# One step less per unit in the chunks, another list of ramp steps, GpSimd in written order from chunk 10 on, the count ahead of the last copies

## The chip, the cores and the metric

The kernel runs on one core of a Trainium2 chip. The metric is the device time of one execution in microseconds, as the median of several runs. An interval or a range of runs stands beside it where there is one.

## What is computed

Three layers follow one another. The first is a recurrence over 768 time steps for each of 4 x 8 heads with a state of 40 x 40; it is shown below with its loop. Its output, 3072 rows of 320 numbers, goes through an expert layer of three products with weights of 320 x 768, of which the largest is taken element by element, and a product back to 320. The last layer has weights of 320 x 2048 and back, with `h * tanh(softplus(h))` between.

```python
for t in range(S):                       # S = 768, heads of 40 x 40
    y[:, :, t] = np.einsum('bhd,bhde->bhe', rt, state)
    Sa = np.einsum('bhde,bhe->bhd', state, at)
    state_decay = state * wt[:, :, None, :] - np.einsum('bhd,bhe->bhde', Sa, bt)
    state = state_decay + np.einsum('bhd,bhe->bhde', vt, kt)
...
h = np.maximum(np.maximum(x @ w1, x @ w2), x @ w3)      # moe1
x = h @ w_out
...
h = x @ w_in                                            # moe2
sp = np.where(h > 20.0, h, np.log1p(np.exp(np.minimum(h, 20.0))))
out = (h * np.tanh(sp)) @ w_out
```

Weights and inputs arrive as 64-bit numbers and are converted on the chip. A value that a product multiplies is held as a high and a low part (names in h and l: bxh and bxl, hh and hl, gh and gl), so that one product of the text is three or more matmuls.

## The kernel before

**The units of work.** The recurrence runs in 48 chunks, c0 to c47. Two successive chunks make a unit, n. `Attention.pre(n)` prepares a unit in steps: each `yield` ends a step, and whoever drives the unit takes one step at a time. The steps are, in order: a scan on VectorE; logarithm and exponential on ScalarE; two steps of VectorE and two more that scale bk; two steps of matmuls (L328) into one PSUM bank of the pool ps_un; the copy ab on ScalarE (L333), which reads half of that bank; the transpose akT on VectorE (L336), which reads the other half; and four selects on GpSimd (L343), which read akT. The transposes kb on TensorE (L388) take banks of the same pool, four to a bank; ScalarE copies them out (L392).

**The solves.** Four units make a batch, and `solve(k)` inverts the triangles of batch k. From the third batch on these are 62 operations on GpSimd, in 31 pairs of a product (L371) and a subtraction (L373), after a transpose on VectorE (L364). For the first two they run on VectorE. `Attention.run` deals the pairs out to the slots that are left until the batch is due.

**The chunks and moe1.** A chunk has five slots. In each, `run` takes a step of the chunk's chain (`chain(c)`, which begins with the copy L452; its TensorE products are cgps, L416, its VectorE copies ud, L464), steps of `moe1.group`, the next unit's steps and steps of the solve. `moe1.group` belongs to four chunks: matmuls bps (L743 to L747), the maximum mx (L873, L875), its high part hh on ScalarE (L877) and its low part hl on GpSimd (L878), which waits for hh; then the output products L916, which need hl, and a copy of the result out (L905, L907). The input bxl is made on VectorE (L756) from the chain's output. L248 is a scaling of ax on GpSimd, and L281 the scan of a later unit.

**What sets the order.** Chunks c0 to c8 come from START, a list of steps that is written out by hand, one token a step: u0 is a step of unit 0, c3 one of chunk 3's chain, e1 one of the solve of batch 1, w5 one of weight tile 5's conversion, f20 a slot of moe1, k6 half of a unit's kb, and further letters are loads and clears. In this ramp all engines keep the written order. From chunk 9 on `run` writes the order; TensorE, VectorE, ScalarE and the DMA queue of SyncE keep it, and GpSimd alone is left to the scheduler:

```python
does = dict(u=unit, x=self.mult, c=chain, e=substitute, ...
...
for x in START.split():
...
                with tc.manual_schedule(engines=IN_ORDER | {mybir.EngineType.Activation}):
                    finish(chunks)
```

**moe2 and the end.** After chunk 47 the rest of moe2's weights is converted, and six groups, `group(q)`, run products (L1093 to L1095), the activation and the products back, in the scheduler's order on every engine. The last group's result leaves in four copies, two on ScalarE and two on VectorE, and two output transfers. Then `gate.count` adds up numbers that ScalarE collected on the way (one matmul, one VectorE reduction and one cast), every engine loads the result into a register (L176) and branches on it (L1363): a slow general version would run only if inputs lay out of bounds.

Of the kernel before, what the change touches and what calls it, by code (L numbers as in the profile page):

```python
# [102 lines left out]
u0 u2 u2 u0 u0 u0 u1 u1 x2 u0 u0 u1 u1 L0 u1 u1 u1 u3 x3 u3 u2 u2 u2 u2 u2 u2 u1 u1 u2 u3 u3 u3 l2 u3 u3 w3 u2
w0 u2 u3 w0 u3 w1 w4 z5 A5 e0 L1 w1 u3 z6 A6 D w2 u3 e0 e0 e0 w5 z4 e0 e0 w1 e0 e0 w3 w0 r V1 e0 z7 A7 A4 e0
w3 e0 w2 e0 e0 w0 e0 e0 w6 e0 e0 K4 K5 U w3 e0 e0 w1 e0 w4 e0 e0 e0 e0 w5 e0 e0 w6 w7 k0 w3 w5 w2 w2 k1 w5 w4
w4 w4 w6 w8 w5 e0 e0 e0 e0 e0 e0 e0 e0 Z0 c0 w7 K6 w7 w6 c0 u4 w8 u4 c0 w9 w6 w10 w8 Z1 x4 w11 w12 w9 c0 w7 u4
u4 w8 V2 c0 w11 w9 w13 u4 u5 w7 L2 w9 c1 A8 w8 w9 w10 w11 w10 k2 w14 w12 w10 u4 u5 x5 c1 w15 u5 w10 w11 u4 u4
w12 w16 c1 w13 w11 w12 w14 c1 w13 w17 w14 u4 w18 u4 w15 w13 c1 u5 w12 k3 V3 w14 u5 K7 w13 w15 w19 w14 u4 w16
u5 L3 w17 w17 u5 c2 w15 w16 w20 c2 u5 w18 c2 w15 w18 w19 u5 w17 w21 u5 c2 V4 c2 w18 k4 w17 u5 w19 w19 w20 c3
w18 w22 w23 w20 L4 w20 K8 w21 c3 w23 w19 w20 c3 w21 w23 w22 k5 w21 c3 w22 w23 w23 A9 u6 w21 V5 w16 c3 w16 L5  # L110
x6 w22 w22 c4 f20 u6 u6 c4 f21 u6 c4 u6 u6 u7 u7 c4 u7 V6 x7 f22 u6 u7 c4 K9 u7 u6 u6 u6 u6 L6 c5 f23 u7 u7 u7
f24 f25 u7 e1 c5 f26 A10 u7 e1 e1 e1 e1 e1 c5 f27 c5 V7 f28 u7 e1 e1 e1 e1 c5 f29 k6 k7 e1 c6 c6 f30 c6 e1 e1
L7 e1 e1 e1 f31 e1 e1 e1 c6 V8 e1 e1 e1 c6 k8 e1 f32 f33 e1 u8 u8 e1 L8 e1 e1 x8 c7 A11 e1 f34 u8 f35 e1 e1 u8
c7 f36 u8 u8 e1 e1 c7 u8 u8 e1 u9 x9 u8 u9 f37 u8 e1 c7 u9 f38 u8 u9 c7 f39 V9 k9 L9 u9 K10 u9 u10 u10 u9 x10
c8 f40 u10 u10 c8 f41 u9 u9 u9 c8 f42 u10 u11 x11 u9 c8 f43 K11 u10 c8 f44 u10 V10 u11 u11 L10
# [1267 lines left out]
```

## Time and profile before

| what | value |
|---|---|
| median of 3 runs | 1033.3 us (1029.38 to 1034.28) |
| the profiled execution, its own time | 1034.91 us |
| the span of its profile | 1033.2 us |
| mean granted TensorE clock | 0.967 |
| TensorE (PE) busy | 917.4 us, 89% |
| VectorE (DVE) busy | 752.2 us, 73% |
| ScalarE (ACT) busy | 735.3 us, 71% |
| GpSimd (POOL) busy | 479.4 us, 46% |

The span runs from the first to the last instruction that the profile holds; the execution's own time is 1.7 us longer. Busy time is summed over an engine's instructions. It is an average over three stages: the ramp (about 0 to 189 us), the chunks (to about 634 us) and moe2 (to the end). A granted clock of 1.0 is 2.4 GHz on TensorE and 0.5 is 1.2 GHz.

### The profile page before, as it was taken

To read this page: it belongs to the slowest core of one execution; us is meant where nothing else is said; L and a number is where in the kernel's file an instruction comes from. 1 tells how busy PE (TensorE), PEld (TensorE's weight loads), DVE (VectorE), ACT (ScalarE), POOL (GpSimd) and SP (SyncE) were. 2 spreads that over 40 slices of the span, in tenths; PEclk is the share of its full clock that TensorE was granted. 3 is DMA by queue.
4 is the path that set the end of the run, shared out by engine and by line. 5 is a ranking of instruction groups with operands and counts; after the bars stand their busy time and mean duration, and the time that the engine had idled before them with its cause. 6 is when DMAs were issued, how large, how long until landed. Compare 5 with 4: busy or idle time off the path is not lost. (4 is left out here: it accounts for less than half of the span.)

```text
span 1033.2 us, 34141 instructions
## 1 busy us (share of the span) xinstructions
PE 917.4 (89%) x14098; PEld 824.6 (80%) x14098; DVE 752.2 (73%) x1411; ACT 735.3 (71%) x1858; POOL 479.4 (46%) x715
## 2 busy tenths in 40 slices
PE   3046778899999999999999999979999999999996
PEld 3034667798888888898988988969888999889985
DVE  8976788665564656565366666698998888898875
ACT  5466635575765667576688977878787978878874
POOL 8488706479659838963953434880202010020000
PEclk9999588899999999999999999989999999999999
DMA  9565522535354454445345454420100000000000
GB/s 233 148 182 160 134 51 65 152 95 150 92 139 118 114 148 106 118 113 139 94 129 151 124 140 150 118 66 1 57 1 31 26 32 26 24 33 1 26 1 29
DMA packets 117334, 96.07 MB, mean 93 GB/s; under 512 B 73316, under 2 KB 93412, under 8 KB 117172
## 3 DMA queue, kind: packets, MB, share of 16 engines
q1 hardware_dynamic: 116432, 93.59, 33.4%
q8 instruction: 113, 1.85, 0.8%
q14 instruction: 49, 0.40, 0.1%
q10 hardware_dynamic: 740, 0.23, 0.1%
HBM read 81.20 MB, written 12.58 MB: 91 GB/s over the span
## 5 line engine op out<-in xcount | busy, mean ns | idle before, releaser
L743 PE MATMUL bps<-bxh,bw 128*128 128x256 f32 x432 | 140.6, 326 | 4.5 <-ACT mx L873 3.4
L744 PE MATMUL bps<-bxl,bw 128*128 128x256 f32 x432 | 124.9, 289 | 3.1 <-DVE bxl L756 3.1
L745 PE MATMUL bps<-bxh,bw 128*128 128x256 f32 x432 | 123.7, 286 | 0.0
L1046 POOL CAST cxh<-cxl 128x512 fp32r<-128x512 f32 x15 | 13.1, 911 | 188.2 <-DMA cxl<-x 188.2
L743 PEld LDWEIGHTS bps<-bxh,bw 128*128 128x128 f32 x432 | 83.4, 193 | 13.3 <-ACT mx L873 4.0
L744 PEld LDWEIGHTS bps<-bxl,bw 128*128 128x128 f32 x432 | 84.2, 195 | 4.9 <-DVE bxl L756 4.9
L248 POOL TENSOR_TENSOR ax<-ax,pp 40x256 f32<-40x256 f32 x96 | 69.2, 739 | 37.1 <-DVE pp L281 24.0
L745 PEld LDWEIGHTS bps<-bxh,bw 128*128 128x128 f32 x432 | 84.1, 195 | 0.0
L483 DVE TENSOR_TENSOR rs<-cgps,cst 64x256 f32<-64x256 f32 x96 | 40.6, 423 | 58.2 <-PE cgps L416 56.1
L878 POOL TENSOR_TENSOR hl<-mx,hh 128x256 fp32r<-128x256 f32 x72 | 56.0, 779 | 52.6 <-ACT hh L877 46.4
L1089 DVE TENSOR_TENSOR gl<-e,gh 128x512 fp32r<-128x512 f32 x93 | 69.9, 752 | 14.4 <-ACT gh L1088 13.4
L500 DVE TENSOR_TENSOR sv<-ys,pp 40x320 f32<-40x320 f32 x92 | 44.9, 488 | 47.3 <-PE ys L495 45.8
L875 DVE TENSOR_TENSOR mx<-bps,mx 128x256 f32<-128x256 f32 x144 | 60.2, 418 | 24.6 <-ACT mx L873 13.7
L373 POOL TENSOR_TENSOR T<-T,tv 128x31 f32<-128x31 f32 (+15 forms) x124 | 73.7, 594 | 8.6
L916 PE MATMUL bps<-hh,bo 128*128 128x256 f32 x360 | 77.0, 296 | 0.6 <-ACT mx L873 0.6
L1077 ACT ACTIVATE e<-e 128x512 f32<-128x512 f32 x93 | 58.6, 630 | 25.4 <-DVE e L1075 25.0
L1081 DVE SCALAR_TENSOR_TENSOR e<-e,r 128x512 f32<-128x512 f32 x93 | 68.6, 737 | 8.7 <-ACT r L1079 8.6
L495 PE MATMUL ys<-rs,ls 128*40 128x72 f32 x1536 | 66.9, 247 | 8.5 <-DVE rs L483 4.2
L371 POOL TENSOR_TENSOR tv<-tr,T 128x31 f32<-128x31 f32 (+15 forms) x124 | 67.8, 547 | 11.1 <-DVE tr L364 2.6
L343 POOL TENSOR_SCALAR_AFFINE_SELECT ax<-akT 32x256 f32<-32x256 f32 x96 | 47.5, 494 | 51.5 <-DVE akT L336 47.3
L495 PEld LDWEIGHTS ys<-rs,ls 128*40 128x40 f32 x1536 | 58.0, 130 | 15.1 <-issue 4.9
L1074 ACT ACTIVATE e<-cps 128x512 f32<-128x512 f32 x93 | 54.7, 589 | 18.9 <-PE cps L747 18.8
(241 smaller groups left out, 3157.2 us busy)
## 6 DMA issues: line engine op xcount, KB each, us to landing
bk<-in_KB_dram SPq DMA_DIRECT2D x24, 448.0 KB
sv<-in_SV_dram SPq DMA_DIRECT2D x96, 80.0 KB
raw<-in_w_dram SPq DMA_DIRECT2D x18, 384.0 KB
again<-in_w_dram SPq DMA_DIRECT2D x27, 256.0 KB
w<-in_W_dram SPq DMA_DIRECT2D x21, 231.0 KB
v<-in_VT_dram SPq DMA_DIRECT2D x48, 96.0 KB
rs<-in_RT_dram SPq DMA_DIRECT2D x48, 96.0 KB
cxl<-x SPq DMA_DIRECT2D x12, 384.0 KB
```

Of the source, the lines that this page charges most:

```text
L248: self.nc.gpsimd.tensor_tensor(out=xv[:, h], in0=xv[:, h], in1=P[ro, h, 0:C], op=ALU.mult)
L371: eng.tensor_tensor(out=tv, in0=abT[:, s, s + 1:C].unsqueeze(2).to_broadcast([128, n, s + 1]), in1=T[:, s, 0:s + 1].unsqueeze(1).to_broadc ...
L373: eng.tensor_tensor(out=T[:, s + 1:C, 0:s + 1], in0=T[:, s + 1:C, 0:s + 1], in1=tv, op=ALU.subtract)
L495: nc.tensor.matmul(out=self.ys[64 * y:64 * y + 40, p, 0:72], lhsT=l[:, y, p], rhs=r_[:, :, 4 * (p % 4) + 2 * (1 - y) + p // 4], start=True ...
L743: nc.tensor.matmul(out=ps, lhsT=h[:, k], rhs=xh[:, k], start=(k == 0), stop=False)
L744: nc.tensor.matmul(out=ps, lhsT=h[:, k], rhs=xl[:, k], start=False, stop=False)
L745: nc.tensor.matmul(out=ps, lhsT=l[:, k], rhs=xh[:, k], start=False, stop=False)
L875: after(1, lambda ps=ps, mx=mx: nc.vector.tensor_tensor(out=mx, in0=ps, in1=mx, op=ALU.max))
L916: nc.tensor.matmul(out=pss[d][rows], lhsT=lhsT, rhs=rhs, start=first, stop=last)
L1077: nc.scalar.activation(out=e, in_=e, func=AF.Square, bias=1.0)
L1081: nc.vector.scalar_tensor_tensor(out=e, in0=e, scalar=1.0, in1=r, op0=ALU.add, op1=ALU.mult)
L1089: nc.vector.tensor_tensor(out=gl, in0=e, in1=gh.bitcast(F32), op=ALU.subtract)
```

## The change

It has four parts.

1. In `pre`, the step between the copy ab and the transpose akT exists only while the ramp is written out (`self.written`). After it, both stand in one step, so akT and the selects come one step earlier.
2. START is another list. It holds the same 472 steps as the one before, in another order. In chunk 9, which `run` writes, the loads of the tests are fixed in order only from there on (`free`).
3. From chunk 10 on (past HAND, 9), a chunk whose number is a multiple of 4 takes no solve steps in its first slot, and from the end of the ramp on GpSimd too keeps the written order.
4. In the last moe2 group, products 13 to 15 are issued one tile earlier; `count` runs ahead of the final copies and takes a bank of the pool psa; three of those copies go to ScalarE and one to VectorE; the second output transfer is issued on ScalarE's queue.

```diff
 START = """
-m0 m1 K0 W0 W1 A0 W2 m2 A2 A1 K1 W3 K2 m3 A3 s1 V0 K3 w0 w1 w2 l1 s0 C l0 p R1 R0 u0 u0 u1 x0 u1 x1 u0 u0 u0
+W0 m1 m2 m0 W1 A2 A0 W2 K0 W3 V0 A1 K1 s0 K2 C m3 A3 s1 K3 w0 w1 w2 l1 p u0 u1 x0 u0 R0 u0 u0 u1 u0 u0 u0 R1
...
-    def count(self):
+    def count(self, psum):
...
-        with self.tc.tile_pool(name="g_ps", bufs=1, space=PSUM) as ps:
-            p = ps.tile([1, len(runs)], F32, name="g_p")
...
+        p = psum[0:1, 0:len(runs)]
+        nc.tensor.matmul(out=p, lhsT=ones, rhs=cnt, start=True, stop=True)
...
         nc.scalar.copy(out=self.ab[:, i:i + 8], in_=psv[:, :, C:2 * C])
-        yield
+        if self.written:
+            yield
         akT = p1.tile([128, 4, 2, C], F32, name="akT")
...
                     steps = -(-left // max(1, 5 * (due - c) - slot - 2))
+                    if c > HAND and c % 4 == 0 and slot == 0:
+                        steps = 0
...
-            self.tc.keep_in_program_order(dma)
+            if self.free:
+                self.tc.keep_in_program_order(dma)
...
+        last = q == 5
...
+        made = {p for r, p in self.ps if r == q}
         for m in range(16 + 3):
-            if early <= m < 16 and (q, m) not in self.ps:
-                self.product(q, m)
+            for p in (m, m + 1)[:1 + (last and m >= 12)]:
+                if early <= p < 16 and p not in made:
+                    self.product(q, p)
+                    made.add(p)
...
+        if last:
+            self.passed = self.gate.count(self.psa.tile([128, self.N], F32, name="cps"))
...
-                if i:
+                if i and not (last and b2):
                     nc.vector.tensor_copy(out=o[:, j], in_=acc[j])
...
-            nc.sync.dma_start(out=self.out[r0:r0 + 2 * GT]...
+            (nc.scalar if last and b2 else nc.sync).dma_start(out=self.out[r0:r0 + 2 * GT]...
...
-                    if c >= HAND and (c > HAND or slot > 0) and slot in (1, 4):
+                    if c >= 9 and (c > 9 or slot > 0) and slot in (1, 4):
...
-                with tc.manual_schedule(engines=IN_ORDER | {mybir.EngineType.Activation}):
+                moe1.free = True
+                with tc.manual_schedule(engines=IN_ORDER | {mybir.EngineType.Activation, mybir.EngineType.Pool}):
...
-    n, total = gate.count()
+    n, total = moe2.passed
```

How the instructions move is shown at three places. The line numbers of the changed kernel are shifted by up to 5: its L883 is L878 of before, its L912 is L907, its L880 is L875, its L247 is L248, and its L745 to L749 are L743 to L747.

**GpSimd, the end of a moe1 group in the chunks (near 330 us).** hl are the low parts that the output products wait for; the rows on T and tv are a solve. Before:

```order
L373 TENSOR_TENSOR T_161<-T_161,tv 128x18x14
L248 TENSOR_TENSOR ax_142<-ax_142,pp_155 40x256 x4
L371 TENSOR_TENSOR tv<-tr_173,T_161 128x255
L878 TENSOR_TENSOR hl_6590<-mx,hh_6584 128x256
L373 TENSOR_TENSOR T_161<-T_161,tv 128x17x15
L371 TENSOR_TENSOR tv<-tr_173,T_161 128x256
L373 TENSOR_TENSOR T_161<-T_161,tv 128x16x16
L371 TENSOR_TENSOR tv<-tr_173,T_161 128x255
L373 TENSOR_TENSOR T_161<-T_161,tv 128x15x17
L878 TENSOR_TENSOR hl_6591<-mx,hh_6585 128x256
L371 TENSOR_TENSOR tv<-tr_173,T_161 128x252
```

With the change, the same stretch of the solve:

```order
L373 TENSOR_TENSOR T_161<-T_161,tv 128x19x13
L371 TENSOR_TENSOR tv<-tr_173,T_161 128x252
L373 TENSOR_TENSOR T_161<-T_161,tv 128x18x14
L883 TENSOR_TENSOR hl_6592<-mx,hh_6586 128x256
L371 TENSOR_TENSOR tv<-tr_173,T_161 128x255
L373 TENSOR_TENSOR T_161<-T_161,tv 128x17x15
L883 TENSOR_TENSOR hl_6593<-mx,hh_6587 128x256
L371 TENSOR_TENSOR tv<-tr_173,T_161 128x256
L373 TENSOR_TENSOR T_161<-T_161,tv 128x16x16
L371 TENSOR_TENSOR tv<-tr_173,T_161 128x255
L373 TENSOR_TENSOR T_161<-T_161,tv 128x15x17
```

The last hl of the group stood behind the pair of operations on 16 x 16 and the pair on 15 x 17. It now stands ahead of both, one pair after the hl before it. The names' numbers are counted otherwise: hl_6593 of after is hl_6591 of before.

**VectorE in the chunks, around a unit's akT (near 290 us).** L907 copies out a result of moe1, L464 is a copy of the chain. Before:

```order
L502 TENSOR_TENSOR YT<-ys,pp_158 104x8x32
L755 TENSOR_SCALAR bxh,g_t<-bxl 128x768
L756 TENSOR_TENSOR bxl<-bxl,bxh 128x768
L907 TENSOR_TENSOR mx<-bps,mx 64x256
L336 STREAM_TRANSPOSE akT<-m_3558 128x2x4x32
L464 COPY ud<-ups 128x4x40
L281 SCALAR_TENSOR_TENSOR pp_157<-w,rst 104x528
```

With the change:

```order
L502 TENSOR_TENSOR YT<-ys,pp_158 104x8x32
L757 TENSOR_SCALAR bxh,g_t<-bxl 128x768
L758 TENSOR_TENSOR bxl<-bxl,bxh 128x768
L336 STREAM_TRANSPOSE akT<-m_3558 128x2x4x32
L912 TENSOR_TENSOR mx<-bps,mx 64x256
L464 COPY ud<-ups 128x4x40
L280 SCALAR_TENSOR_TENSOR pp_157<-w,rst 104x528
```

akT stood behind L907 and now stands ahead of it; the rows above and below keep their order.

**TensorE in chunk 9, just past the ramp.** L388 are the transposes kb, L743 to L747 a group of moe1 products, L472 and L416 are of the chain. Before:

```order
L746 MATMUL bps<-bxh,bw_107 128x256
L747 MATMUL bps<-bxl,bw_107 128x256
L472 MATMUL utps<-cst,ud 128x128 x2
L743 MATMUL bps<-bxh,bw_108 128x256
L744 MATMUL bps<-bxl,bw_108 128x256
L745 MATMUL bps<-bxh,bw_108 128x256
L743 MATMUL bps<-bxh,bw_108 128x256
L744 MATMUL bps<-bxl,bw_108 128x256
L745 MATMUL bps<-bxh,bw_108 128x256
L746 MATMUL bps<-bxh,bw_108 128x256
L747 MATMUL bps<-bxl,bw_108 128x256
L388 MATMUL kb<-cst,bk_150 128x104 x8
```

With the change:

```order
L388 MATMUL kb<-cst,bk_150 128x104 x4
L472 MATMUL utps<-cst,ud 128x128 x2
L745 MATMUL bps<-bxh,bw_108 128x256
L746 MATMUL bps<-bxl,bw_108 128x256
L747 MATMUL bps<-bxh,bw_108 128x256
L745 MATMUL bps<-bxh,bw_108 128x256
L746 MATMUL bps<-bxl,bw_108 128x256
L747 MATMUL bps<-bxh,bw_108 128x256
L748 MATMUL bps<-bxh,bw_108 128x256
L749 MATMUL bps<-bxl,bw_108 128x256
L388 MATMUL kb<-cst,bk_150 128x104 x4
L416 MATMUL cgps<-rs_167,uT 32x32
```

The eight transposes stood in one row behind the products. Four of them now stand ahead of L472 and of the products, and four behind these.

## Rows read from the trace of the kernel before

**Rows 1.** The page, busy time of each engine over the span.
```profile
PE 917.4 (89%) x14098; PEld 824.6 (80%) x14098; DVE 752.2 (73%) x1411; ACT 735.3 (71%) x1858; POOL 479.4 (46%) x715
```

**Rows 2.** Busy time by stretch: us, each engine (x), PEclk, DMA share, GB/s.
```profile
123.00:158.00 35.00, 26.50 (x504) 23.76 (x504) 30.88 (x76) 13.62 (x41) 7.63 (x13) 0.80 0.26 57
...
290.00:339.00 49.00, 46.53 (x1017) 42.58 (x1018) 28.53 (x53) 31.27 (x97) 41.69 (x66) 0.93 0.45 119
...
740.00:1000.00 260.00, 260.00 (x1436) 234.09 (x1435) 226.54 (x373) 216.80 (x373) 22.19 (x18) 1.00 0.07 23
```

**Rows 3.** Waits of TensorE from 189 to 634 us: total, times, longest.
```profile
PE kb L388 <- DVE akT L336: 4.7, 6, 1.0
...
PE bps L916 <- POOL hl L878: 3.2, 3, 1.5
...
PE cgps L416 <- ACT uT L475: 2.5, 3, 1.4
```

**Rows 4.** Busy time and granted clock (PEclk) of two short stretches, as in rows 2.
```profile
197.00:203.80 6.80, 6.17 (x130) 5.46 (x132) 1.87 (x4) 3.13 (x10) 2.70 (x6) 0.50 0.32 89
...
425.70:429.10 3.40, 3.40 (x56) 3.04 (x45) 0.78 (x2) 0.00 (x0) 3.02 (x5) 0.50 0.15 46
```

**Rows 5.** Timeline near 290 us: start, length, instruction [idle before <-what ended it].
```profile
289.59 0.36 ACT L333 COPY ab<-m 128x256 f32<-128x256 f32 x1
...
291.09 0.42 DVE L907 TENSOR_TENSOR mx<-bps,mx 64x256 f32<-64x256 f32 x1 [1.13 <-ACT mx L905]
...
291.55 0.45 DVE L336 STREAM_TRANSPOSE akT<-m 128x256 f32<-128x256 f32 x1
...
292.15 0.55 PE L388 MATMUL kb<-cst,bk 104*128 104x104 f32 x4 [1.02 <-DVE akT L336]
```

**Rows 6.** Timeline near 330 us, GpSimd (POOL) and TensorE.
```profile
328.08 0.62 POOL L371 TENSOR_TENSOR tv<-tr,T 128x256 f32<-128x256 f32 x1
...
330.93 0.72 POOL L878 TENSOR_TENSOR hl<-mx,hh 128x256 fp32r<-128x256 f32 x1
...
331.70 0.38 PE L916 MATMUL bps<-hl,bo 128*128 128x256 f32 x1 [1.42 <-POOL hl L878]
```

**Rows 7.** Groups of GpSimd by line in the chunks; lengths ns min/median/max of akT, hl.
```profile
L373 POOL TENSOR_TENSOR T<-T,tv 128x31 f32<-128x31 f32 (+15 forms) x124 | 73.7, 594 | 8.6
...
L371 POOL TENSOR_TENSOR tv<-tr,T 128x31 f32<-128x31 f32 (+15 forms) x124 | 67.8, 547 | 11.1 <-DVE tr L364 2.6
...
L343 POOL TENSOR_SCALAR_AFFINE_SELECT ax<-akT 32x256 f32<-32x256 f32 x57 | 29.5, 517 | 43.6 <-DVE akT L336 41.4
...
L336 DVE STREAM_TRANSPOSE akT<-m x14: 439/441/451, 194.1 to 477.9; 128x256 f32<-128x256 f32 x14
...
L878 POOL TENSOR_TENSOR hl<-mx,hh x59: 722/734/1687, 201.6 to 631.6; 128x256 fp32r<-128x256 f32 x59
```

**Rows 8.** Timeline of chunk 9 near 197 us.
```profile
194.56 0.57 PE L388 MATMUL kb<-cst,bk 104*128 104x104 f32 x4 [0.64 <-DVE akT L336]
...
196.73 0.85 ACT L392 COPY ls<-kb 64x320 f32<-64x320 f32 x2
...
197.63 0.95 PE L388 MATMUL kb<-cst,bk 104*128 104x104 f32 x4 [2.50 <-ACT ls L392]
```

**Rows 9.** Timeline of the end.
```profile
1023.16 0.41 PE L1093 MATMUL cops<-c_cw,gh 128*128 128x320 f32 x1 [1.34 <-ACT gh L1088]
...
1024.44 0.75 PE L1095 MATMUL cops<-c_cw,gl 128*128 128x320 f32 x4
...
1026.54 0.14 DVE L175 CAST g_n<-g_s 1x1 int32<-1x1 f32 x1
```

**Rows 10.** Register load (L176) and branch (L1363) by engine: lengths ns min/median/max.
```profile
L176 PEldq TENSOR_LOAD <-g_n x1: 1033/1033/1033, 1026.7 to 1026.7; - x1
...
L1363 ACTq COMPARE_BRANCH  x1: 50/50/50, 1027.7 to 1027.7; - x1
...
L1363 PEldq COMPARE_BRANCH  x1: 4012/4012/4012, 1027.9 to 1027.9; - x1
```

More of the change, by code (lines that the diff above doesn't have):

```diff
@@ L101 @@
 START = """
-m0 m1 K0 W0 W1 A0 W2 m2 A2 A1 K1 W3 K2 m3 A3 s1 V0 K3 w0 w1 w2 l1 s0 C l0 p R1 R0 u0 u0 u1 x0 u1 x1 u0 u0 u0
[L103 to L115, printed above, removed]
+W0 m1 m2 m0 W1 A2 A0 W2 K0 W3 V0 A1 K1 s0 K2 C m3 A3 s1 K3 w0 w1 w2 l1 p u0 u1 x0 u0 R0 u0 u0 u1 u0 u0 u0 R1
@@ new lines @@
+u2 x1 u2 l0 u1 u1 u2 u0 x2 u1 u1 u0 u1 u0 u0 u1 u1 u3 x3 u3 l2 u2 u2 u2 L0 u1 u3 u1 u3 z6 u3 u3 u2 u2 u2 u3 w0
+w3 L1 u2 u2 u3 w1 w1 u3 e0 w0 w4 w5 u3 z4 u3 z5 w2 K4 e0 A5 e0 w1 e0 e0 e0 A6 z7 e0 U A4 e0 w0 w0 A7 w2 w3 e0
+e0 w6 e0 e0 e0 w1 w4 w3 w3 w5 K5 e0 e0 e0 e0 e0 e0 w3 e0 e0 e0 w7 w2 w2 w4 w4 w5 w4 w6 e0 k0 k1 e0 w6 D w8 w5
+e0 w5 r K6 w9 w10 e0 V1 e0 e0 e0 e0 e0 e0 e0 e0 c0 w7 w7 Z0 c0 u4 w8 w8 u4 c0 w9 w11 w12 x4 w7 c0 u4 u4 w9 Z1
+w8 V2 w13 w11 c0 u4 w7 w8 L2 w9 c1 A8 w6 w11 w6 u5 w10 w10 u4 k2 w12 w10 x5 w13 u5 u5 u5 w10 w12 u4 u4 w14 w11
@@ new lines @@
+w11 w13 c1 c1 w9 c1 w15 w16 w17 u4 u4 w13 w13 V3 w14 w14 w18 w12 k3 w12 u5 u5 w15 c1 L3 w17 w15 w19 w14 w16 c2
+c2 w14 u4 w15 w18 w18 u5 c2 w17 w19 u5 w15 w16 w20 w21 c2 V4 w19 w18 u5 w17 u5 w19 w20 w18 u5 w22 w17 c2 k4
+w23 w20 c3 A9 L4 c3 w20 w21 w23 w19 w21 c3 w20 w22 w23 w22 w22 w21 k5 w23 c3 V5 w21 u6 w16 w22 w16 c3 L5 w23
+K7 c4 f20 u6 u6 c4 x6 u6 c4 u6 f21 u6 u7 u7 K8 c4 u7 u7 u6 c4 L6 u6 u7 u6 u6 x7 V6 u6 c5 u7 u7 u7 f22 f23 u7
+A10 f24 f25 K9 c5 u7 u7 e1 e1 e1 e1 e1 e1 c5 c5 e1 f26 f27 e1 e1 e1 V7 f28 k6 c5 L7 e1 e1 e1 e1 c6 c6 e1 c6 e1
@@ L116 @@
+k7 c6 e1 e1 e1 f29 e1 e1 f30 e1 c6 L8 f31 f32 u8 f33 e1 e1 u8 e1 e1 c7 A11 f34 f35 e1 u8 u8 x8 V8 e1 e1 e1 u8
+u8 c7 e1 e1 f36 c7 u8 u8 u8 e1 u9 x9 u9 u8 f37 k8 e1 c7 u9 V9 f38 u8 u9 c7 K10 f39 u9 u9 u10 x10 u10 u10 u9 c8
+L9 f40 c8 u10 u9 u9 f41 u9 u10 u11 c8 f42 x11 c8 V10 f43 u10 k9 K11 c8 u9 u10 f44 u11 u11 L10
 """
@@ L168, in count @@
         nc.vector.memset(ones, 1.0)
-        with self.tc.tile_pool(name="g_ps", bufs=1, space=PSUM) as ps:
-            p = ps.tile([1, len(runs)], F32, name="g_p")
-            nc.tensor.matmul(out=p, lhsT=ones, rhs=cnt, start=True, stop=True)
-            s = pool.tile([1, 1], F32, name="g_s")
-            nc.vector.tensor_reduce(out=s, in_=p, op=ALU.add, axis=mybir.AxisListType.X)
+        p = psum[0:1, 0:len(runs)]
+        nc.tensor.matmul(out=p, lhsT=ones, rhs=cnt, start=True, stop=True)
+        s = pool.tile([1, 1], F32, name="g_s")
+        nc.vector.tensor_reduce(out=s, in_=p, op=ALU.add, axis=mybir.AxisListType.X)
         n = pool.tile([1, 1], I32, name="g_n")
@@ L802, in weights @@
             yield from64(self.nc, self.tmp, self.A["wo"][j], 1, DM, self.gate, lambda t, j=j: self.put_out(t[:, 0], j), later=True)
+    free = False
     def tests(self):
@@ L1133, in group @@
             r0 = (2 * ga + b2) * S + sb * GT
-            nc.sync.dma_start(out=self.out[r0:r0 + 2 * GT].rearrange("(i p) d -> p i d", i=2), in_=o[:, b2:4:2])
+            (nc.scalar if last and b2 else nc.sync).dma_start(out=self.out[r0:r0 + 2 * GT].rearrange("(i p) d -> p i d", i=2), in_=o[:, b2:4:2])
 def any64(nc, pool, src, n, cols, out):
```

## The prediction

> **What bounds the kernel now.** I read the page first, then busy time by stretch, then who makes TensorE wait in the chunks, then the granted clock behind those waits, and last the end of the program instruction by instruction. TensorE is busy for 89% of the span [rows 1]. By stretch it falls into three parts [rows 2]. In the ramp no engine is full for long; VectorE comes nearest, with 30.88 of 35 us from 123 to 158 us, where the second solve runs on it. In the chunks TensorE is the bound: 46.53 of 49 us from 290 to 339 us, with GpSimd second at 41.69. In the closing stage TensorE is simply full, 260.00 of 260 us. So a wait of TensorE in the chunks is worth its own length, while in the ramp only the chain through the list counts.
>
> In the chunks TensorE's waits are few and have names [rows 3]: the transposes kb (L388) wait for VectorE's akT, 4.7 us in six places; the output products L916 wait for GpSimd's hl, 3.2 us in three; cgps (L416) waits for ScalarE's uT, 2.5 us. One kb waits 2.50 us for ScalarE's copies of the kb before it [rows 8]. The reader should add what comes behind some of them: near 197, 262, 293, 334 and 426 us, each time within two and a half microseconds of such a wait, the granted clock stands at 0.50, that is 1.2 GHz, for 6.8 us the first time and 3.4 us the other four, with TensorE nearly full [rows 4], which shows the first and the last of the five. At half the rate 3.4 us do the work of 1.7, so such a stretch costs 1.7 us beside the wait, the long one 3.4.
>
> **The change, part by part.**
>
> *akT one step earlier.* akT now shares its slot with ab, the ScalarE copy that empties the same bank. Before, VectorE took L907 first; L907 waited for ScalarE until 291.09 us, akT followed at 291.55, and kb came 1.02 us late, although ab had begun at 289.59 [rows 5]. After, akT stands ahead of L907, so it need not wait for what L907 waits for. No instruction is added. L907 becomes later by akT's length, 0.45 us; behind it is an output transfer, for which TensorE does not wait. At most all six waits go, 4.7 us, and the clock stretch near 293, 1.7 us; at least nothing. I take 4.1 + 1.7 = 5.8 us, and leave out the wait of 0.64 us at 194.56 [rows 8], the one of the six in the part that the list reorders.
>
> *GpSimd in written order, and no solve steps in the first slot of every fourth chunk.* The last hl of a group stood behind four solve operations, the first of them at 328.08 us; it ran at 330.93 us and TensorE's product came 1.42 us late [rows 6]. Now it stands ahead of those four: a lead of 330.93 - 328.08 = 2.85 us against a wait of 1.42. One group later the same pattern costs the longest wait of its row, 1.5 us [rows 3]. Both waits go, 2.9 us, with their two clock stretches, 3.4 us: 6.3 us, at least nothing. The solve operations left out of that slot go to others. Counted from the order, two successive chunks held up to 26 of them on GpSimd and now hold 20 in the steady pattern; at 0.57 us each, the mean of their two lines [rows 7], the fullest pair gives up 6 x 0.57 = 3.4 us of GpSimd work. A pair lasts (477.9 - 194.1) / 13 = 21.8 us by the starts of akT [rows 7]. That is why I expect no new queue in the steady pattern. The first solve in the chunks keeps 26 operations in a pair, and there, near 259 us, an hl that holds back ScalarE now stands behind more work than before: for the uT wait I count nothing.
>
> *The list of ramp steps.* It holds the same 472 steps, so the engines do the same work. Until the first solve ends VectorE has the same seven weight conversions ahead of it, so chunk 0 starts when it did, and up to chunk 7 VectorE's work only moves from one chunk to the next. I take 0, and as bounds 8 us either way, twice the 4 us that VectorE is idle in the stretch of rows 2. One edit is plain: in chunk 9 eight kb transposes stood in a row on one bank, and the second four waited 2.50 us until ScalarE had copied the first four, which it did only at 196.73 us [rows 8]. They now stand apart, with a group of products between them. That wait and the 6.8 us at half clock would go: 2.5 + 3.4 = 5.9 us, at least nothing; I take it all.
>
> *The end.* TensorE waited 1.34 us for the last gh [rows 9]. In the last group, products 13 to 15 are now issued one tile early, so ScalarE and VectorE get their inputs earlier while TensorE's own work stays: I take 1.2 us, bounds 0 and 1.34. After that, TensorE's last products ended at 1024.44 + 0.75 = 1025.19 us; copies, the count's matmul and its cast (1026.54 + 0.14) followed, then a register load of 1.033 us and a branch of 4.012 us on TensorE [rows 9, 10]. So the branch could not begin before 1026.68 + 1.03 = 1027.7 us, 2.5 us behind the last product. Now the count runs among the last products and only the load, 1.03 us, stands between: 1.5 us gained, bounds 0 (if another engine's branch ends last) and 1.5. The output transfer that moves to ScalarE's queue I give nothing, since the branch outlasts it. Together 2.7 us.
>
> The branch costs what its row shows, 4.012 us [rows 10]. The Trainium skill (Advanced Engine Details and Errata, Control Flow Timing) gives a compare-and-branch about 108 ns. By that figure the end would already be 3.9 us shorter and the kernel now near 1029; on TensorE the trace does not agree, on ScalarE, where the same branch took 50 ns, it nearly does, and the rows decide.
>
> **The sum.** 5.8 + 6.3 + 5.9 + 0 + 2.7 = 20.7 us if nothing comes back. Something does: a TensorE that runs earlier meets ScalarE, VectorE and the transfers where they were. I take 60% of the chunk part, 0.6 x 18.0 = 10.8, between 0 and all, nearer to all because in each place the order shows the late instruction moved; and the end in full: 13.5 us. The profiled execution took 1034.9 us (span 1033.2 and 1.7 around it), 1.6 above the median of the three runs, 1033.3. 1034.9 - 13.5 is 1021.4, on the median's footing 1019.8. I say **1020.5**.
>
> **The rivals.**
>
> *More, 1009.* All 18.0 us of the chunk part come, and the list brings 3 us as well: 1033.3 - 18.0 - 2.7 - 3 = 1009.6. For it: each edit sits at a named wait. Against: behind one wait another usually stands. Chance 0.18.
>
> *The waits only change their name, 1030.* akT is early, but kb then waits for ab or for the copies of the kb before; hl is early, but TensorE waits for hh. Only the end stays: 1033.3 - 2.7 = 1030.6. For it: ab had begun only 1.96 us ahead of akT [rows 5]. Against: it takes 0.36 us there, and kb came 2.6 us after it began. A second way to this time is an hl that gets longer where it now runs: one took 1.687 us where the median is 0.734 [rows 7], 0.95 us more, which alone is within the lead of 2.85. The Trainium skill (SBUF — State Buffer, Who interferes with whom) states that a GpSimd operation and a VectorE operation with two SBUF inputs hold each other off for a whole instruction; by that rule the new order would draw such pairs anew in every chunk. The long hl agrees with it, but no row here shows the cause. Chance 0.20.
>
> *Slower, 1042.* A queue in written order stops at its first instruction that isn't ready. GpSimd stood idle for 41.4 us in front of its selects (L343), waiting for akT [rows 7]; the scheduler had put other work ahead of them. If hl now queues behind such a select, a group pays what rows 3 and 4 show for one hl wait, 1.4 + 1.7 = 3.1 us. With eight of ten groups hit: 8 x 3.1 = 24.8, less the 6.3 paid already, is 18.5; the other gains stay, 0.6 x 11.7 + 2.7 = 9.7: 1033.3 + 18.5 - 9.7 = 1042.1. It decides as soon as a select waits longer than hl's lead of 2.85 us. Against: akT itself comes earlier. Chance 0.10. That the change doesn't do what it says is excluded by the order.
>
> **How the numbers follow.** The forecast has 0.52 (its own range 1014 to 1027), more 0.18, renamed waits 0.20, slower 0.10. The range, 1009 to 1034, leaves out half of the first rival and the slow one. A measurement of this kernel can tell about 0.5%, 5.2 us, so faster means below 1028.1: the forecast, the first rival and a little of the second, 0.73; no change 0.17; slower 0.10.
>
> **What would show it.** Right: after 200 us no kb waits for akT and no L916 for hl; the stretches at half clock behind those waits are gone, and the clock over the span rises above its mean before; TensorE's branch begins about 1.1 us after its last product. Wrong: GpSimd idle in front of L343 while an L916 waits; a chunk 9 that starts its first copy later than before; new kb waits with ScalarE's name.

## The result

The changed kernel takes 1021.85 us (median of 4 runs, 1019.84 to 1023.65) beside 1033.74 for the kernel before in the same session: a ratio of 0.9894, interval 0.9861 to 0.9926. The forecast was 1020.5. One of the eight runs of the list alone, further down, took 1441.17 us at a mean granted clock of 0.592, and no ratio below contains it, though the median there does. Of the 13.2 us by which the profiled span shrank (1033.2 to 1020.0), this is where they lie, by the start of a chunk's first copy (L452), in us:

| | c9 | c10 | c12 | c13 | c15 | c17 | c29 | c47 | end of span |
|---|---|---|---|---|---|---|---|---|---|
| before | 188.9 | 207.5 | 229.2 | 240.8 | 267.5 | 289.8 | 431.3 | 624.5 | 1033.2 |
| changed | 188.7 | 204.9 | 226.6 | 246.0 | 268.5 | 290.1 | 422.7 | 615.4 | 1020.0 |
| difference | -0.2 | -2.6 | -2.6 | +5.2 | +1.0 | +0.3 | -8.6 | -9.1 | -13.2 |

The ramp gave nothing, chunk 9 gave 2.4 us, chunk 12 lost 7.8, the chunks from 13 to 47 won it back and 6.5 more, and what comes after chunk 47 gave 4.1. Two profiles of one code differ by a few of these: in the kernel below that changes the end alone, whose chunks are those of before, chunks 9 to 47 took 2.4 us less than in the profile of before.

Busy time over the span, to hold against [rows 1]:

```profile
PE 913.2 (90%) x14098; PEld 822.3 (81%) x14098; DVE 749.6 (73%) x1410; ACT 736.1 (72%) x1859; POOL 479.1 (47%) x715
```

The work is the same. What changed is in the waits of TensorE from 189 to 634 us, as in [rows 3]:

```profile
PE bps L921 <- POOL hl L883: 4.8, 1, 4.8
...
PE bps L746 <- DVE bxl L758: 2.5, 8, 0.6
...
PE m L327 <- POOL ax L247: 2.0, 1, 2.0
...
PE cgps L416 <- ACT uT L475: 1.1, 2, 0.6
```

No kb waits for akT any more, and the waits for hl near 331 and 424 us are gone. In their place stands a single wait for hl of 4.8 us, one for ax of 2.0, and the old ones for bxl and uT (1.1 us, where it was 2.5). The timeline around the long one, on ScalarE, GpSimd and TensorE:

```profile
224.23 0.41 ACT L882 CAST hh<-mx 128x256 fp32r<-128x256 f32 x1
...
226.91 3.62 POOL L247 TENSOR_TENSOR ax<-ax,pp 40x256 f32<-40x256 f32 x4
...
234.82 0.72 POOL L883 TENSOR_TENSOR hl<-mx,hh 128x256 fp32r<-128x256 f32 x1
...
235.60 0.58 PE L921 MATMUL bps<-hl,bo 128*128 128x256 f32 x1 [4.78 <-POOL hl L883]
```

The high part hh was ready at 224.23 + 0.41 = 224.64 us. The hl made from it ran at 234.82, 10.2 us later. GpSimd had worked almost without a pause (gaps of 0.08 us at most) through what stood ahead of it: the scaling of ax and operations of the first solve in the chunks, of which 28 all told stand ahead of this hl. Before the change the same hl, the third of its group, ran 2.65 us after its hh, behind 19 of them. TensorE waited 4.78 us, and its work behind the wait ran at half rate. Busy time by stretch shows it, with the columns of [rows 2]:

```profile
189.00:240.00 51.00, 44.20 (x996) 40.18 (x996) 27.60 (x53) 30.25 (x93) 37.48 (x60) 0.90 0.45 116
...
234.20:242.50 8.30, 6.90 (x163) 6.22 (x165) 0.84 (x2) 0.37 (x1) 7.75 (x12) 0.50 0.11 33
...
240.00:290.00 50.00, 49.49 (x1131) 45.08 (x1132) 29.03 (x59) 33.58 (x103) 30.75 (x53) 0.96 0.46 122
...
290.00:339.00 49.00, 48.35 (x1085) 44.02 (x1085) 32.36 (x59) 34.60 (x106) 42.75 (x66) 1.00 0.52 135
...
740.00:1000.00 260.00, 260.00 (x1438) 234.17 (x1436) 225.71 (x372) 215.99 (x371) 21.65 (x18) 1.00 0.06 20
```

From 234.20 to 242.50 us the granted clock is 0.50, 1.2 GHz, with TensorE nearly full from 235.60 on; in the trace the half rate begins at 233.3, within the wait, and ends at 243.5. 7.9 us of work at half rate cost 3.9 us beside the wait's 4.78. From 290 to 339 us, by contrast, the clock is 1.00 and TensorE busy for 48.35 of 49 us, where it was 46.53 at a clock of 0.93 [rows 2]. In moe2 TensorE is full as before, 260.00 of 260 us.

The end of the program, first TensorE's last two groups of products, then the branch (L1375) by engine with ns and first and last start:

```profile
1011.69 0.41 PE L1098 MATMUL cops<-c_cw,gh 128*128 128x320 f32 x1
...
1012.96 0.75 PE L1100 MATMUL cops<-c_cw,gl 128*128 128x320 f32 x4
```

```profile
L1375 SPq EVENT_SEMAPHORE  x8: 17/17/17, 1017.9 to 1018.6; - x8
...
L1375 PEldq COMPARE_BRANCH  x1: 3452/3452/3452, 1013.0 to 1013.0; - x1
...
L1375 SPq COMPARE_BRANCH  x1: 50/50/50, 1014.6 to 1014.6; - x1
```

The wait of 1.34 us for the last gh [rows 9] is gone. The last product ended at 1012.96 + 0.75 = 1013.71 us, and the span 6.3 us later, at 1020.0; before, it was 1033.2 - 1025.19 = 8.0 us.

### The profile page after: what moved, and what is told of

Its sections match the earlier page's. It is cut to its first block, busy times and chain, and to the rows that moved or that the text cites. A ratio compares the mean times of both kernels' runs of the same rounds, so it can differ in the third digit from the quotient of the medians.

```text
span 1020.0 us, 34114 instructions
## 1 busy us (share of the span) xinstructions
PE 913.2 (90%) x14098; PEld 822.3 (81%) x14098; DVE 749.6 (73%) x1410; ACT 736.1 (72%) x1859; POOL 479.1 (47%) x715
## 4 chain that ended last, share of the span: by engine, by line
PE 67%; DVE 12%; ACT 8%; DMA 4%; POOL 4%; issue 3%; SPq 1%; DVEq 0%; POOLq 0%; ACTq 0%
PE bps L745 6%; PE cops L1098 5%; PE cops L1099 5%; PE cops L1100 5%; PE ys L495 5%; PE cps L745 4%; PE cps L746 4%; PE cps L747 4%; PE bps L746 4%; PE bps L747 4%; PE bps L921 3%; PE cgps L416 2%; PE ups L462 2%; PE cps L749 2%; PE cps L748 2%
## 5 line engine op out<-in xcount | busy, mean ns | idle before, releaser
L745 PE MATMUL bps<-bxh,bw 128*128 128x256 f32 x432 | 140.2, 325 | 2.3 <-ACT mx L878 1.8
L747 PE MATMUL bps<-bxh,bw 128*128 128x256 f32 x432 | 123.6, 286 | 0.0
L745 PEld LDWEIGHTS bps<-bxh,bw 128*128 128x128 f32 x432 | 83.3, 193 | 11.1 <-ACT mx L878 2.2
L883 POOL TENSOR_TENSOR hl<-mx,hh 128x256 fp32r<-128x256 f32 x72 | 57.3, 796 | 66.9 <-ACT hh L882 61.9
L747 PEld LDWEIGHTS bps<-bxh,bw 128*128 128x128 f32 x432 | 84.0, 194 | 0.0
L247 POOL TENSOR_TENSOR ax<-ax,pp 40x256 f32<-40x256 f32 x96 | 68.7, 734 | 21.9 <-PE m L327 5.6
L880 DVE TENSOR_TENSOR mx<-bps,mx 128x256 f32<-128x256 f32 x144 | 60.2, 418 | 19.5 <-ACT mx L878 10.8
L495 PE MATMUL ys<-rs,ls 128*40 128x72 f32 x1536 | 64.7, 243 | 8.5 <-ACT bw L690 4.7
L1079 ACT ACTIVATE e<-cps 128x512 f32<-128x512 f32 x93 | 54.7, 589 | 18.6 <-PE cps L749 18.5
```

The source lines that it names most:

```text
L247: self.nc.gpsimd.tensor_tensor(out=xv[:, h], in0=xv[:, h], in1=P[ro, h, 0:C], op=ALU.mult)
L495: nc.tensor.matmul(out=self.ys[64 * y:64 * y + 40, p, 0:72], lhsT=l[:, y, p], rhs=r_[:, :, 4 * (p % 4) + 2 * (1 - y) + p // 4], start=True ...
L745: nc.tensor.matmul(out=ps, lhsT=h[:, k], rhs=xh[:, k], start=(k == 0), stop=False)
L747: nc.tensor.matmul(out=ps, lhsT=l[:, k], rhs=xh[:, k], start=False, stop=False)
L880: after(1, lambda ps=ps, mx=mx: nc.vector.tensor_tensor(out=mx, in0=ps, in1=mx, op=ALU.max))
```

## The experiments

Each kernel ran in one of three sessions beside the kernel before; the ratios are to that kernel's runs of the same session.

| run | what it is | median us | ratio, 95% interval |
|---|---|---|---|
| e1_akt | akT alone | 1022.75 | 0.9899, 0.9881 to 0.9917 |
| e2_gps | GpSimd's part alone | 1032.30 | 0.9986, 0.9970 to 1.0003 |
| e3_list | the list alone | 1029.45 | 0.9962, 0.9945 to 0.9979 |
| e4_end | the end alone | 1030.88 | 0.9977, 0.9961 to 0.9992 |
| e5_sched | all, GpSimd by the scheduler | 1019.87 | 0.9883, 0.9862 to 0.9905 |
| e6_noskip | all, no slot left out | 1025.47 | 0.9922, 0.9901 to 0.9943 |
| e8_late | all, first solve late | 1021.30 | 0.9889, 0.9866 to 0.9912 |
| e9_oldlist | all but the list | 1019.15 | 0.9864, 0.9846 to 0.9882 |
| e10_mix | written order from c17 on | 1015.05 | 0.9820, 0.9801 to 0.9839 |
| e11_mix_oldlist | that, with the old list | 1011.99 | 0.9811, 0.9788 to 0.9834 |
| e7_even | all, first solve even | 1020.67 | 0.9888, 0.9862 to 0.9913 |
| e12_again | the change once more | 1023.00 | 0.9892, 0.9872 to 0.9913 |

Two things can be read from the runs together. First, akT alone (0.9899) can't be told from the whole change (0.9894 and 0.9892). Alone the four parts gained 10.4, 1.4, 3.9 and 2.4 us by their ratios, 18.1 in sum; together they gained 11. Second, in each trace the stretch from the start of chunk 9 to that of chunk 47 is TensorE's work at full rate, 407 to 410 us, and two additions: the time in which TensorE is idle, and half of the time that it stands at 1.2 GHz. In us:

| | c9 to c47 | TensorE idle | at 1.2 GHz |
|---|---|---|---|
| before | 435.6 | 16.7 | 20.5 |
| the end alone (chunks as before) | 433.2 | 16.8 | 13.7 |
| GpSimd's part alone | 435.2 | 17.8 | 17.1 |
| the list alone | 430.8 | 15.9 | 10.2 |
| akT alone | 426.7 | 12.7 | 10.2 |
| the change | 426.7 | 12.7 | 13.7 |
| all, GpSimd by the scheduler | 424.1 | 11.5 | 6.8 |
| written order from c17 on | 419.4 | 8.9 | 3.4 |

The first two rows run the same code in the chunks, so the time at 1.2 GHz can differ by 6.8 us without a cause in the program: the wait for uT of 1.40 us near 259 us has 3.4 us at half rate behind it in the one and none in the other.

### The four parts alone

The theory was that each part removes the waits it is named for, and that GpSimd's long wait comes of the first solve in the chunks. The rivals stand with each run.

**akT alone.** To the kernel before:

```diff
         nc.scalar.copy(out=self.ab[:, i:i + 8], in_=psv[:, :, C:2 * C])
-        yield
+        if self.written:
+            yield
```

> Only the first part: akT one step earlier in the chunks; list, GpSimd and the end as before. Theory (each part removes the waits it is named for): of the six waits of kb for akT (4.7 us) at least the five behind 200 us go, with the half-rate stretch near 293 us; the hl waits near 331 and 424 us (1.42 and 1.49 us) and the kb wait for ls near 197 us (2.50 us) stay. Time 2 to 6 us under the kernel before, 1028 to 1032. Rival (the waits change their name): kb then waits for ScalarE's copies, time within 1 us of before, 1033 to 1035.

Measured: 1022.75 us, 10.4 less by the ratio, far more than either theory gave. The waits of TensorE in the chunks:

```profile
PE bps L917 <- POOL hl L879: 5.0, 3, 2.2
...
PE m L328 <- POOL ax L248: 2.0, 1, 2.0
...
PE cgps L417 <- ACT uT L476: 1.1, 2, 0.6
```

All six waits for akT are gone, the hl waits stayed (and grew from 1.5 to 2.2 us), as expected. Chunks 9 to 47 take 426.7 us, as long as in the changed kernel. Not expected: the kb wait of 2.50 us near 197 us [rows 8] is gone too. The eight kb of chunk 9 run in two groups of four here, at 191.7 and 193.2 us. A unit blocks the kb from the start of its matmuls to akT (`held`); with akT a slot earlier the first half is let through a slot earlier. A new wait has come in the same chunk:

```profile
197.61 1.04 PE L328 MATMUL m<-bk,ax 40*32 40x64 f32 x32 [2.04 <-POOL ax L248]
```

This wait for ax of 2.0 us stands in all ten profiles with this part, GpSimd in written order or not, and in none of the others. So the one wait was traded for the other, and chunk 9 gained less than was lifted.

**GpSimd alone.**

```diff
+                    if c > HAND and c % 4 == 0 and slot == 0:
+                        steps = 0
...
-                with tc.manual_schedule(engines=IN_ORDER | {mybir.EngineType.Activation}):
+                with tc.manual_schedule(engines=IN_ORDER | {mybir.EngineType.Activation, mybir.EngineType.Pool}):
```

> Only the third part: GpSimd in written order and no solve steps in the first slot of every fourth chunk; akT, list and end as before. Theory (the dealing of the first solve in the chunks overfills GpSimd, whoever else changes): the hl waits near 331 and 424 us go with their stretches at half rate (6.3 us), and a wait of 2 to 5 us for hl appears near 236 us, since hl there now stands behind 26 solve operations where it stood behind 19, with half rate after it; net time 1029 to 1034. Rival (the new wait of the changed kernel needs the earlier akT or the list): no hl wait over 1 us near 236 us, time 1026 to 1029.

Measured: 1032.30 us, a ratio of 0.9986 whose interval holds 1.

```profile
PE bps L918 <- POOL hl L880: 5.4, 3, 3.6
...
PE kb L388 <- DVE akT L336: 3.4, 6, 0.7
...
PE kb L388 <- ACT ls L392: 2.5, 1, 2.5
```

The wait near 424 us is gone and the one near 331 shrank to 0.76 us, but two waits of 3.57 and 1.04 us stand near 240 us, with half rate from 240.6 to 247.5: from chunk 12 to 13 this kernel takes 18.6 us where the one before took 11.6. From c17 to c47 it gains 2.9 us; one stretch at half rate is left there, at 428.3 us, behind a wait of 0.93 that has no named cause. The long wait needs neither the early akT nor the list, and the rival falls.

**The list alone.** Only the text of START and the flag `free` are those of the change.

> Only the list of ramp steps; akT, GpSimd and the end as before. Theory: chunk 9's first copy starts within 2 us of the 188.9 us of before, the kb wait of 2.50 us near 197 us goes, and another wait of about 2 us near 198 us does not come, since the scheduler still pulls GpSimd's scaling of ax ahead of the selects; then the stretch at half rate goes too, and chunk 10 starts 4 to 6 us earlier; time 1027 to 1030. Rival (the list itself moves TensorE's wait): a wait for ax near 198 us as in the changed kernel, chunk 10 starts 2 to 3 us earlier, time 1030 to 1032.

```profile
PE kb L388 <- DVE akT L336: 4.5, 6, 1.0
...
PE bps L919 <- POOL hl L881: 3.5, 3, 1.6
...
PE kb L388 <- ACT ls L392: 2.5, 1, 2.5
```

Measured: 1029.45 us, a ratio of 0.9962. The time lies in the theory's range, but not for its reason: the kb wait for ls of 2.5 us is still there, and the rival's wait for ax isn't. The list does not part the kb of chunk 9. Chunk 9 even starts 0.9 us later. In this profile the chunks are shorter by the clock: 10.2 us at half rate, where the profile before has 20.5 and that of the end alone 13.7. Whether the list causes this is not shown.

**The end alone.** The hunks of `count`, `group` and the last lines, as in the diff of the change.

> Only the end: products 13 to 15 one tile early, the count ahead of the last copies, three copies on ScalarE, the second transfer on ScalarE's queue. Theory (the end stands by itself): the wait of 1.34 us for the last gh falls under 0.3 us, and from the last product to the end of the span pass 6.3 us where it was 8.0; time 2.5 to 3.5 us under the kernel before, 1030 to 1031.5. Rival (the end gained only because TensorE arrived in another phase of the scheduler's order): less than 1.5 us gained.

```profile
L1368 SPq EVENT_SEMAPHORE  x8: 17/17/17, 1023.6 to 1024.4; - x8
...
L1368 PEldq COMPARE_BRANCH  x1: 3435/3435/3435, 1018.7 to 1018.7; - x1
```

Measured: 1030.88 us, 2.4 less by the ratio, just under the 2.5 expected. TensorE waits for no gh over 0.1 us; its last product ends at 1018.64 + 0.75 = 1019.39 us and the span at 1025.8, 6.4 us later. The end stands by itself.

### GpSimd's order, with everything else changed

**The scheduler again.**

```diff
-                with tc.manual_schedule(engines=IN_ORDER | {mybir.EngineType.Activation, mybir.EngineType.Pool}):
+                with tc.manual_schedule(engines=IN_ORDER | {mybir.EngineType.Activation}):
```

> The changed kernel, but GpSimd is left to the scheduler in the chunks, as before the change. Theory (in the first solve of the chunks GpSimd has more work than time, and written order leaves hl behind 28 of its operations where the scheduler leaves it behind 19): the hl wait of 4.78 us near 236 us falls under 1 us, two hl waits of 1.5 to 2.2 us come back near 325 and 415 us, and the time is 1015 to 1019 us. Rival (with akT early and the list, the scheduler's order is as slow): 1021 us or more.

```profile
PE bps L921 <- POOL hl L883: 4.2, 3, 2.2
```

Measured: 1019.87 us, between the theory's range and the rival's; the ratio, 0.9883, can't be told from the changed kernel's. The wait near 236 us is 0.65 us, the later ones are back with 1.43 and 2.17 us, each with half rate behind it. From c12 to c13 it takes 11.9 us, where the changed kernel takes 19.4; from c17 to c47 its gain on the kernel before is 3.5 us, against the changed kernel's 9.4. So each order wins in one stretch about what it loses in the other.

**No slot left out.** The line `steps = 0` and its condition are taken out.

> The changed kernel, but the first slot of every fourth chunk takes solve steps again. Theory (the left-out steps are what keeps the last hl of a group in time): that hl then stands behind 2 more operations, 1.3 us; waits of 0.4 to 1.5 us for it appear near 327 and 415 us, each with a stretch at half rate, and the wait near 236 us is followed by another; time 1022 to 1027. Rival (written order alone does it): time within 1 us of the changed kernel's 1021.9, no hl wait over 0.3 us behind 300 us.

```profile
PE bps L919 <- POOL hl L881: 7.1, 4, 4.9
```

Measured: 1025.47 us. The four waits are 4.93, 0.36, 0.89 and 0.89 us, the last two near 332 and 421 us, where 0.4 to 1.5 was expected. No half rate followed them. From c17 to c47 it takes 327.5 us, the changed kernel's two profiles 325.3 and 325.5: the left-out slot is worth those two waits. By the medians alone the two kernels could not be told apart, since the intervals overlap.

**The first solve dealt more slowly, and dealt evenly.** To the changed kernel, for the one and for the other:

```diff
+                    if k == 2 and (c < 12 or (c + slot) % 2):
+                        steps = min(steps, 1)
```

```diff
+                    if k == 2 and c < 13 and (slot + c) % 2:
+                        steps = min(steps, 1)
```

> The changed kernel, with the first solve in the chunks dealt more slowly: one pair a slot at most up to chunk 11, and one or two in turn after it. Written order stays. The hl that waited then stands behind 14 operations where it stood behind 28. Theory (GpSimd is overfilled there): the wait of 4.78 us and the half rate behind it go, chunk 13 starts 6 to 8 us earlier against chunk 12 than in the changed kernel, and no hl wait over 1 us takes their place; time 1013 to 1017. Rival (written order itself, an instruction that is not ready at the head of GpSimd's queue): a wait for hl over 2 us stays near 236 us, time 1020 or more.

> The changed kernel in written order, with the first solve dealt evenly: one pair and two pairs in turn up to chunk 12, so that the hl which waited stands behind 22 solve operations where it stood behind 28, and the hl of chunk 13 behind as many as in the changed kernel. Theory (six operations of 0.6 us less ahead of it): the wait of 4.78 us shrinks by 3 to 4 us, to about 1 us; nothing new over 1.5 us up to 280 us, since the solve ends when it did; time 1015 to 1019. Rival (any work put off comes back as a wait of ScalarE, VectorE or TensorE, as in the slower dealing): waits of 2 us or more between 250 and 280 us, 1020 to 1023.

Measured: 1021.30 and 1020.67 us; neither can be told from the changed kernel, and both theories missed the time. The hl wait near 236 us is gone in the first and 0.68 us in the second, as expected, and chunk 13 starts 8.1 and 5.4 us earlier than in the changed kernel. The rival of the even dealing, that work put off comes back as a wait, is borne out, with 1.83 us for uT where 2 or more was expected. TensorE's waits of the two, in this order, are

```profile
PE cgps L416 <- ACT uT L475: 3.8, 3, 2.6
...
PE ys L495 <- DVE rs L483: 2.6, 1, 2.6
```

```profile
PE cgps L416 <- ACT uT L475: 2.9, 3, 1.8
...
PE bps L923 <- POOL hl L885: 0.7, 1, 0.7
```

By chunk 15 or 16 the gain is given back: from chunk 10 to 17 the two take 85.3 and 85.4 us, the changed kernel 85.2. The timeline of the slow dealing shows how:

```profile
255.39 0.72 POOL L885 TENSOR_TENSOR hl<-mx,hh 128x256 fp32r<-128x256 f32 x1
...
256.15 0.37 ACT L880 COPY mx<-bps 128x256 f32<-128x256 f32 x1 [4.39 <-POOL hl L885]
...
256.42 0.76 ACT L475 COPY uT<-utps 40x256 f32<-40x256 f32 x2
...
256.83 0.24 PE L416 MATMUL cgps<-rs,uT 40*32 40x32 f32 x2 [2.64 <-ACT uT L475]
```

A later hl is now the late one: it stands behind 40 operations and runs at 255.39 us, 8.1 us after its hh. ScalarE's copy mx writes what hl reads and waits 4.39 us for it; uT stands behind mx in ScalarE's queue, and TensorE behind uT, again with half rate after it. The wait of 2.58 us for rs is VectorE's, which is held at the solve's end by its transpose (L377) of GpSimd's last result. So less work ahead of one hl is more ahead of another: in this stretch GpSimd has next to no free time (21.30 of 23 us from 213 to 236 us in the changed kernel, the line below), and none of the three dealings in written order found a place for the solve.

**Both orders, each in its place.** To the changed kernel:

```diff
-            if c == HAND:
+            if c in (HAND, 17):
                 yield
...
                 moe1.free = True
+                with tc.manual_schedule(engines=IN_ORDER | {mybir.EngineType.Activation}):
+                    next(chunks)
                 with tc.manual_schedule(engines=IN_ORDER | {mybir.EngineType.Activation, mybir.EngineType.Pool}):
```

> The changed kernel, but GpSimd is left to the scheduler up to chunk 16, where the first solve in the chunks ends, and keeps the written order from chunk 17 on. Theory (the scheduler's order is better where GpSimd has too much work, the written one where it has enough time): no hl wait over 1 us near 236 us, and none over 0.3 us from 300 to 634 us; up to chunk 17 it gains as the variant with the scheduler alone, about 9 us against the changed kernel, and keeps it; time 1012 to 1016 us. Rival (what the first solve loses is paid later anyway, at its end): a wait of TensorE for ScalarE's uT or VectorE's rs of over 1.5 us between 250 and 280 us, time 1018 or more.

```profile
PE bps L746 <- DVE bxl L758: 3.0, 9, 0.7
...
PE m L327 <- POOL ax L247: 2.0, 1, 2.0
...
PE bps L921 <- POOL hl L883: 0.2, 1, 0.2
```

The same hl, the third of its group, and busy time from 213 to 236 us, first of the changed kernel, then of this one, with the columns of [rows 2]:

```profile
226.51 0.41 ACT L882 CAST hh<-mx 128x256 fp32r<-128x256 f32 x1
...
228.20 1.19 POOL L883 TENSOR_TENSOR hl<-mx,hh 128x256 fp32r<-128x256 f32 x1
```

```profile
213.00:236.00 23.00, 18.23 (x354) 16.59 (x349) 10.99 (x22) 14.36 (x45) 21.30 (x34) 0.94 0.45 121
...
213.00:236.00 23.00, 22.32 (x519) 20.10 (x521) 12.68 (x26) 15.65 (x48) 21.36 (x36) 1.00 0.42 106
```

Measured: 1015.05 us, faster than both kernels (0.9820, the changed kernel in the same session 0.9892). No wait for hl over 0.3 us is left, and none for uT or rs over 0.7, unlike in the two dealings. From c9 to c17 it takes 6.8 us less than the changed kernel's first profile, where about 9 was expected. GpSimd is as full as there, 21.36 of 23 us, yet TensorE is busy for 22.32 where it was 18.23, and the transpose at the solve's end starts at 268.4 us (272.7 in the changed kernel). The hl that ran 10.2 us after its hh runs 1.3 us after it, behind 18 operations of the solve. So it is the order, not the amount of work: the scheduler's sequence has an hl ahead of solve operations where the written one has it behind. Whether a list written by hand with the scheduler's sequence would do as well was not tried.

### The list again

For these two only START is that of the kernel before, in the changed kernel and in the mixed one.

> The changed kernel with the list of ramp steps of before. Theory (the list is worth beside the others what it was alone, 3.6 us): 1024 to 1027. Rival (its gain alone came from runs that differ in TensorE's clock in the ramp, or is swallowed by the wait for GpSimd in the first solve): within 1.5 us of 1021.9. In either case the kb wait of 2.5 us near 197 us stays away, since akT's step moves it and not the list.

> As the run before it in this list, with the list of ramp steps of before. If the list is worth 3.6 us, as it seemed alone, 3 to 5 us slower than that run; if it costs 2.7 us, as it seemed beside the other parts, 2 to 4 us faster; if it does nothing, within 1.5 us of it.

> The changed kernel itself, once more, beside the three others. Expected 1020 to 1024 us, with the hl wait of 4 to 5 us near 236 us; where TensorE's clock in the ramp from 90 to 132 us differs from the first profile, chunk 9's first copy may start up to 2.5 us apart.

Measured: 1019.15 us without the new list, beside 1021.85 and 1023.00 with it, below both expected ranges; the kb wait of 2.5 us stays away, as expected; 1011.99 beside 1015.05 in the mixed kernel, where the ranges (1011.10 to 1016.33, 1013.17 to 1015.79) overlap and the ratios (0.9811, 0.9820) can't be told apart. Alone the list gained 3.9 us, beside the others it seems to cost about 3. In the profiles the start of chunk 9 differs less than this: 187.1 to 191.5 us in six with the old list (mean 188.5), 188.0 to 191.7 in eight with the new (mean 189.7); the two profiles of the changed kernel alone lie 3.0 us apart. What the list does, and why its sign turns, stays open; that the result does not need it is shown. The changed kernel's long wait came again, with 4.83 us. The lowest median is that of the mixed kernel with the old list.

## Why the prediction was right, and where it was right by luck

**akT one step earlier: right, and undersized.** The step moved what it named. But the prediction gave "That wait and the 6.8 us at half clock" of chunk 9 to the list of ramp steps: this step failed. The part that removes the wait is akT's, through `held`; the list alone leaves it. Of the 5.9 us, 2.5 came: the mean from c9 to c10 is 16.0 us in ten profiles with akT's part (the changed kernel's two among them) and 18.5 in the four without, since the wait for ax took its place. The clock was undersized too: the sum gave akT one stretch at half rate, 1.7 us, while its own profile has 10.2 us at half rate from c9 to c47 where 20.5 stood before, worth 5.1 us, beside 4.0 us less idle time. Up to 3.4 us of those 5.1 lie within what two profiles of one code differ by. The part alone is worth 10.4 us, where 5.8 stood in the sum.

**GpSimd in written order: right behind chunk 17, wrong ahead of it.** The 6.3 us for the two hl waits and their half rate were met beside the early akT: from c17 to c47 the mixed kernel gains 9.9 us on the kernel before and the one with the scheduler's order 3.5, which makes 6.4. Alone, the part gained 2.9 there. The step that failed is "for the uT wait I count nothing", and the sentence ahead of it: the prediction saw that the first solve in the chunks keeps 26 operations in a pair of chunks and that an hl there "now stands behind more work than before", and priced it at nothing. The hl that it named, near 259 us, cost nothing: no wait for uT stands there any more. The one that came late was another, near 236 us, and it cost 7.8 us from c12 to c13.

**The list in the ramp: 0 expected.** Chunk 9 starts 0.2 us earlier in the changed kernel's first profile and 2.9 later in its second, within what profiles of one list differ by.

**The end: right in size, one step wrong, so by luck in part.** 1.34 us of gh wait went (1.2 in the sum), and 1.7 us between the last product and the end (1.5 in the sum). The other 1.2 us behind chunk 47 lie ahead of the moe2 groups, in the stage from 634 to 690 us, and stood in no step. But TensorE's branch does not come "about 1.1 us after its last product": the register load ran while products were still running and the branch began at 1013.04 us, 0.67 us ahead of the last product's end. It took 3.45 us and ended at 1016.5. What ends last is SyncE, which branches behind its output transfer, at 1014.6, starts its next instruction at 1017.9 and works through semaphores until 1019.2. It ended last before the change too: its branch stood at 1028.0 and its next instruction at 1031.3, and its semaphores ran to 1032.4, when TensorE's branch was over (1031.9). So the 1.7 us came from SyncE, which branches 0.9 us behind the last product where it was 2.8, and not from TensorE's branch, by which the 1.5 had been worked out.

**The discount of 60%, and the luck.** It was meant for a TensorE that meets the others where they were, and no row stood behind its size. From c9 to c47 the profiles gave 8.9 us of 18.0, half, but not by general friction: one queue took 7.8 us back, and the rest of the chunks gave 16.7. That the forecast of 1020.5 lies so near the measured 1021.85 is luck in this: akT's part gave nearly twice its price, and beside it the list and GpSimd's part gave nothing net in the chunks (426.7 us from c9 to c47 with akT alone and with all four), since the loss of the first solve, which stood in no term, ate what written order won behind it. The last 0.7 us, from the sum's 1019.8 to 1020.5, have no term either.

**The rivals.** "The waits only change their name" held in one chunk (ax for ls). "Slower" named the right engine and the right kind, hl in a queue in written order, but another head of the queue: while the one late hl waited, GpSimd did not stand idle ahead of a select; it was working on the solve. The second way of the renamed waits, an hl that gets longer, can be seen in the rows but did not matter: in the first profiles of the two kernels six hl between 189 and 634 us took 1.18 to 1.69 us, each beside a VectorE operation with two inputs (pp, bk or Q), in five of the six begun 0.13 to 0.41 us earlier; TensorE waited for none of the six. The expected rise of the mean clock did not come in the first profile (0.959 after 0.967), since a stretch of the ramp was at half rate.

## What to carry to other kernels

A written order served GpSimd where it had time to spare: it put the urgent operation ahead. Where GpSimd was full for a stretch, three dealings of the work in written order each made some urgent operation late, and the scheduler's order took 6.7 us less from chunk 10 to 17 (78.5 for 85.2). So split the program by stages and try each order in each. Price a wait with its clock: here idle time and half of the time at half rate explained the whole stage to within 3 us. Parts that gain 18.1 us one by one can gain 11 together, so run each alone: one of the four was worth as much as all. And before a removed wait is credited to one edit, ask which flag or buffer let the waiting instruction through: here it was in another part of the diff.
